# A fused attention, soft-MoE and MLP kernel: its opening stretch rearranged

## The chip, the cores and the metric

The kernel runs on one core of a Trainium2 chip. The time is device microseconds (us) of one launch. The kernel before has a median of 685.09 us over 3 runs (683.9 to 685.98). The names of the engines are those of the profile: PE is TensorE (PEld its weight loads), DVE VectorE, ACT ScalarE, POOL GpSimd, SP the engine whose queue issues the transfers (DMA).

## The reference

Three layers follow one another. What is computed, cut to its core:

```python
# attention: q, k, v (4, 12, 448, 64); rmsnorm(x, g) = x / sqrt(mean(x*x) + 1e-6) * g
q_n, k_n = rmsnorm(q, g_q), rmsnorm(k, g_k)
scores = q_n @ k_n.T / sqrt(64);  scores -= scores.max(-1)
attn = exp(scores);  attn /= attn.sum(-1) + 1e-9;  x = attn @ v      # -> (1792, 768)
# soft MoE: 8 experts, 4 slots each, phi (768, 32), w1 (8, 768, 1024), w2 (8, 1024, 768)
logits = x @ phi;  d = softmax(logits, axis 0);  c = softmax(logits, axis 1)
h = relu((d.T @ x)[expert] @ w1[expert]);  x = c @ (h @ w2[expert])
# MLP: w_in (768, 2048), w_out (2048, 768), given in 64 bit and narrowed on the chip
h = x @ w_in;  g = max(h, 0) + alpha * min(h, 0);  out = g @ w_out
```

## The kernel before

The 48 heads are worked in 24 pairs; two pairs make a group, and q and k of a group come in one tile `qk` (load_qk, one transfer of 448 KB for q and one for k, two such tiles). For each pair n:

- norm_sum 0 squares q and k on ACT into the tile `sqr` (of which there is one buffer, NSQ = 1), norm_sum 1 sums the squares on DVE. norm_rs makes the inverse roots `y` of a whole group: a logarithm and an exponential on ACT, then four small steps on DVE.
- split_mul writes the normed tile `nf` in three products: k by the gains (w = 1), q by its roots (w = 0), k by its roots (w = 2). The gains `G` are the product of g_q and g_k. split_hi rounds `nf` to 16 bits on ACT, split_lo subtracts that from `nf` (the rest). Which engine does the three products and the two subtractions is in the table "PMUL": before, POOL does all five of every pair. There is one `nf` buffer (NNF = 1), so pair n+1's first product waits for pair n's last subtraction.
- turn transposes the split tile on PE (7 matmuls for q, 7 for k), turned copies it out of PSUM on ACT, and transfers bring a second copy to `qB` and `kB`; twin does the same for q. rowmax_mm (PE) and rowmax (DVE) take the row maxima, turn_m and turned_m put them into a row of `qB`.
- score_mm makes the scores on PE, score the exponentials on ACT (two of each block, three blocks of seven with a rest on POOL or DVE by score_lo), and av the products with v on PE. av_out divides.

While the pairs run, the MoE steps of finished pairs, the fetches of w1 and w2 (`unit<-in_moe_w_dram`) and of w_in, and the narrowing of w_in are put between. After the last pair come the experts, whose weights are read from HBM, and the MLP.

The work of all 24 pairs is a list `plan` of 2374 events, and the tuple ORDER gives their order. Each engine takes its instructions strictly in that order, and the SP queue its transfers too: an instruction that waits holds up all behind it on its engine. Ahead of the plan stand the constants: `ident` (POOL), `stack` and `ident16` (DVE), then setup_constants(0), which writes the constant rows 64 to 66 of `qB[0]` and `kB[0]` on POOL. The first event of the plan is setup_constants(1): DVE copies these rows to the other two `qB` and `kB`, and sets `dT`, `vH` and `vR`.

## Time and profile before

| | us |
|---|---|
| median of 3 runs | 685.09 (683.9 to 685.98) |
| the profiled execution, its own time | 685.34 |
| its span, first to last instruction | 683.6 |
| PE busy in the span | 618.2 |
| DVE busy | 456.5 |
| ACT busy | 367.2 |
| POOL busy | 187.9 |

The span is what the profile shows instruction by instruction; 1.74 us of the profiled time lie outside of it. Times of the trace are us from the span's start. In the rows a group names line, engine, operation, output<-input by the program's names, and shape. "x2" is a count; what stands in brackets is how long the engine sat idle before, and what ended that.

### The profile page before, as it was taken

The numbers are of one execution on the slowest core, as the hardware profiler recorded it, in microseconds if no ns is written. First come the engines' busy times: TensorE is split into PE (matmuls) and PEld (weight loads), VectorE is DVE, ScalarE is ACT, GpSimd is POOL, SyncE is SP. The second block draws the span as 40 slices with busy tenths as digits, with TensorE's granted clock in tenths as the row PEclk, the third lists the DMA queues.
The fourth block names the chain that finished last, engine by engine and source line by source line (L and its number), as shares of the span: only waits on it lengthen the run. The fifth ranks groups of instructions, "written<-read, shape, count | busy, mean of one in ns | idle before, by whom it ended". The sixth has DMA issues, their size and how long they took to land.

```text
span 683.6 us, 14138 instructions
## 1 busy us (share of the span) xinstructions
PE 618.2 (90%) x5670; PEld 478.2 (70%) x5670; DVE 456.5 (67%) x913; ACT 367.2 (54%) x709; POOL 187.9 (27%) x195
## 2 busy tenths in 40 slices
PE   0799998889999999997988468999999999999997
PEld 0367766666767776775333114888899999999997
DVE  5778999898999998853011154999964545454540
ACT  3799998798999997771112223776521111111110
POOL 6967665556648562321010000000000000000000
PEclk9989999999999999999999959999999999999999
DMA  4565677462636523669899999330020101010101
GB/s 138 132 204 181 191 206 210 126 174 62 196 97 189 146 62 98 180 211 423 350 424 423 425 425 423 108 120 0 1 93 1 46 1 47 1 47 0 47 1 46
DMA packets 36240, 106.89 MB, mean 156 GB/s; under 512 B 5448, under 2 KB 22352, under 8 KB 31824
## 3 DMA queue, kind: packets, MB, share of 16 engines
q1 hardware_dynamic: 36176, 106.01, 44.4%
q8 instruction: 44, 0.72, 0.5%
q14 instruction: 20, 0.16, 0.1%
HBM read 92.18 MB, written 5.51 MB: 143 GB/s over the span
## 4 chain that ended last, share of the span: by engine, by line
PE 61%; ACT 16%; DMA 9%; DVE 6%; POOL 4%; issue 3%; SPq 0%; DVEq 0%; ACTq 0%; POOLq 0%
PE psa L1491 12%; PE psa L1492 12%; PE psa L1490 11%; DMA unit<-in_moe_w_dram 7%; PE psn L783 5%; PE psv L843 3%; ACT e L799 3%; PE psv L833 3%; PE psa L1332 2%; PE psr L765 2%; PE psa L1303 2%; ACT psn L804 2%; ACT sp L688 2%; POOL nf L682 2%; ACT e L797 1%
## 5 line engine op out<-in xcount | busy, mean ns | idle before, releaser
L1490 PE MATMUL psa<-whi,gh 128*128 128x384 f32 (+1 forms) x448 | 152.0, 339 | 0.0
L1491 PE MATMUL psa<-wlo,gh 128*128 128x384 f32 (+1 forms) x448 | 151.1, 337 | 0.0
L1492 PE MATMUL psa<-whi,gl 128*128 128x384 f32 (+1 forms) x448 | 150.8, 337 | 0.0
L774 DVE TENSOR_REDUCE m<-psr 128x1 f16<-128x448 f32 x168 | 97.5, 615 | 5.7 <-PE psr L765 5.5
L1459 ACT CAST gh<-t 128x512 fp32r<-128x512 f32 x40 | 24.9, 621 | 123.0 <-DVE t L1456 122.5
L1492 PEld LDWEIGHTS psa<-whi,gl 128*128 128x128 f32 x448 | 84.1, 188 | 2.8
L1491 PEld LDWEIGHTS psa<-wlo,gh 128*128 128x128 f32 x448 | 84.2, 188 | 2.7
L1490 PEld LDWEIGHTS psa<-whi,gh 128*128 128x128 f32 x448 | 84.2, 188 | 2.7
L843 PE MATMUL psv<-vH,e 128*128 128x65 f16 (+1 forms) x1152 | 84.8, 195 | 0.0
L843 PEld LDWEIGHTS <-e 128*128 128x128 f16 (+1 forms) x1728 | 80.1, 106 | 0.0
L1453 DVE TENSOR_SCALAR t<-pst,alpha_t 128x256 f32<-128x256 f32 x80 | 34.9, 477 | 62.9 <-PE pst L1447 62.9
L815 POOL TENSOR_TENSOR e<-ef,e 128x448 f16<-128x448 f32 x48 | 53.3, 1111 | 81.3 <-ACT ef L804 60.2
L833 PEld LDWEIGHTS psv<-vR,e 128*128 128x128 f32 (+1 forms) x384 | 59.5, 178 | 20.7 <-issue 11.4
L843 PE MATMUL psv<-vL,e 128*128 128x64 f16 (+1 forms) x576 | 73.0, 194 | 0.0
L799 ACT ACTIVATE e<-psn 128x448 f16<-128x448 f32 x120 | 65.1, 542 | 13.1 <-PE psn L783 10.6
L783 PE MATMUL psn<-q,k 128*128 128x448 f16 (+1 forms) x192 | 62.9, 370 | 9.1 <-ACT ef L804 3.1
L833 PE MATMUL psv<-vR,e 128*128 128x65 f32 (+1 forms) x384 | 70.2, 264 | 0.2 <-PE psn L783 0.2
L783 PE MATMUL psn<-qB,kB 67*128 67x448 f16 (+1 forms) x192 | 62.4, 365 | 1.2 <-DMA qB<-mr 1.2
L765 PE MATMUL psr<-k,q 128*128 128x448 f16 (+1 forms) x192 | 59.1, 383 | 3.8 <-ACT k L717 2.8
L695 POOL TENSOR_TENSOR sp<-nf,sp 128x448 f16<-128x448 f32 x48 | 50.2, 1055 | 12.1 <-ACT sp L688 10.7
L815 DVE TENSOR_TENSOR e<-psn,e 128x448 f16<-128x448 f32 x72 | 44.3, 616 | 13.2 <-ACT psn L804 12.9
L710 PE MATMUL pst<-ident,sp 128*128 128x128 f16 x336 | 28.2, 232 | 17.5 <-POOL sp L695 17.4
(170 smaller groups left out, 1069.6 us busy)
## 6 DMA issues: line engine op xcount, KB each, us to landing
unit<-in_moe_w_dram SPq DMA_DIRECT2D x26, 1536.0 KB, 16.4
unit<-in_moe_w_in_dram SPq DMA_DIRECT2D x24, 512.0 KB, 5.7
rawo<-in_moe_w_out_dram SPq DMA_DIRECT2D x8, 1536.0 KB, 14.5
unit<-in_moe_w_dram SPq DMA_DIRECT2D x36, 256.0 KB, 5.1
qk<-in_q_dram SPq DMA_DIRECT2D x12, 448.0 KB, 3.9
qk<-in_k_dram SPq DMA_DIRECT2D x12, 448.0 KB, 5.8
out_dram<-osb SPq DMA_DIRECT2D x14, 384.0 KB, 2.3
vR<-in_v_dram SPq DMA_DIRECT2D x24, 128.0 KB, 3.9
```

The lines of the kernel that those rows point to most:

```text
L695: eng.tensor_tensor(out=d["sp"][:, a, :, D:], in0=d["nf"][:, a], in1=d["sp"][:, a, :, 0:D], op=ALU.subtract)
L765: nc.tensor.matmul(pn[o0:o1, :S], d["q"][:, c0 : c0 + o1 - o0], d["k"][:, h * S : (h + 1) * S], start=True, stop=True)
L774: nc.vector.tensor_reduce(out=d["m"][:, c : c + 1], in_=d.pop(("pn", c))[:, :S], axis=AX.X, op=ALU.max)
L783: nc.tensor.matmul(pe[o0:o1, :S], lhs[:, c0 : c0 + o1 - o0], rhs[:, h * S : (h + 1) * S], start=st_, stop=not st_,)
L799: nc.scalar.activation(e2[:, 0], pe[:, :S], AF.Exp, scale=0.125)
L815: eng.tensor_tensor(out=e2[:, 1], in0=ef, in1=e2[:, 0], op=ALU.subtract)
L833: nc.tensor.matmul(pv[o0:o1, slot, :], d["e", c][:, qs], d["vv"][:, h, sl * D : 4 * D + 1], start=(j == 0), stop=False,)
L843: nc.tensor.matmul(pv[o0:o1, slot, 0:wd], d["e", c][:, w // 2, qs], (vl if w == 1 else vh)[:, 4 * h + sl, 0:wd], start=(j == 0 and w == 0) ...
L1453: nc.vector.tensor_scalar(out=t0[:, cs], in0=ph[:, cs], scalar1=0.0, scalar2=alpha_t[:, f // 2, i : i + 1], op0=ALU.min, op1=ALU.mult)
L1490: nc.tensor.matmul(a, gh[f][:, ms], hi[:, hs], start=(f == 0 and not (packed and m % 2 == 1 and hf == 0)), stop=False)
L1491: nc.tensor.matmul(a, gh[f][:, ms], lo[:, hs], start=False, stop=False)
L1492: nc.tensor.matmul(a, gl[f][:, ms], hi[:, hs], start=False, stop=(f == KF - 1 and not (packed and m % 2 == 0 and hf == 1)))
```

## The change

Six things are changed.

1. PMUL_OF: all five split steps of pair 0 go to DVE. Pairs 1 to 23 stay on POOL.
2. The constant rows of `qB[0]` and `kB[0]` are written by DVE. The two other copies are made by four small transfers on the SP queue. `vH` and `vR` are set in an event of their own (part 2), `dT` and `stack` in another (part 3), both later in the order.
3. NSQ is 2: two `sqr` buffers.
4. The gains g_q and g_k are fetched first, on ACT's queue, no longer between the two `qk` groups on SP's.
5. NWARM = 12 events of 4 matmuls each on constants (`ident16` by 256 columns of `ident`), into a PSUM buffer that nothing reads. 6 of these events stand ahead of the first transposes.
6. ORDER has 14 more events (2 of constants, 12 of the matmuls). Its first 405 events are in another order (419 with the new ones); from there to the end it is the same.

```diff
-    NSQ = 1
+    NSQ = 2
+    NWARM = 12
...
-    nc.vector.tensor_reduce(
-        out=stack[:, 0, :], in_=ident.rearrange("p (g s) -> p s g", g=4), axis=AX.X, op=ALU.add
-    )
-    for r in range(1, 4):
-        nc.vector.tensor_copy(stack[:, r, :], stack[:, 0, :])
...
             r = qB[0]
-            nc.gpsimd.memset(r[D : D + 3], FC_C)
+            nc.vector.memset(r[D : D + 3], FC_C)
...
-            fc_rows(nc.gpsimd, 0)
-            return
-        got.add("const")
-        for ts in (qB, kB):
-            for t in ts[1:]:
-                if ts is qB or FCS[1] == FCS[2] == FCS[0]:
-                    nc.vector.tensor_copy(t[D : D + 3], ts[0][D : D + 3])
...
+            fc_rows(nc.vector, 0)
+        elif part == 1:
+            got.add("const")
+            for ts in (qB, kB):
+                for t in ts[1:]:
+                    nc.sync.dma_start(t[D : D + 3], ts[0][D : D + 3])
+            nc.sync.dma_start(phi_sb, phi.rearrange("(t p) s -> p t s", p=P))
+        elif part == 2:
+            for t in vH:
...
+            got.add("const v")
+        else:
+            nc.vector.memset(dT[:, S : 4 * P + D], 0.0)
+            nc.vector.tensor_reduce(
...
+    def warm_up(i):
+        if not warm:
+            warm.append(psv())
+        for _ in range(4):
+            nc.tensor.matmul(warm[0][:, : 2 * P], ident16, ident.bitcast(F16), start=True, stop=True)
...
+    def PMUL_OF(n):
+        return {0: ()}.get(n, T["PMUL"][n % 2])
...
-        eng = nc.gpsimd if w in T["PMUL"][n % 2] else nc.vector
+        eng = nc.gpsimd if w in PMUL_OF(n) else nc.vector
...
+        gqk = small.tile([P, 2, D], F32, tag="gqk", name="gqk", bufs=1)
+        nc.scalar.dma_start(gqk[:, 0, :], g_q.rearrange("(o d) -> o d", o=1).to_broadcast([P, D]))
+        nc.scalar.dma_start(gqk[:, 1, :], g_k.rearrange("(o d) -> o d", o=1).to_broadcast([P, D]))
         setup_constants(0)
...
-        gqk = small.tile([P, 2, D], F32, tag="gqk", name="gqk", bufs=1)
-        nc.sync.dma_start(gqk[:, 0, :], g_q.rearrange("(o d) -> o d", o=1).to_broadcast([P, D]))
```

Three places in the engines' order show what moved.

On DVE, at the opening, before: the last constants, then the sums of squares (L641, into `u`), the four small steps of the roots (L654 to L661), the next two sums and the first row maxima (L774).

```order
L582 MEMSET vR_123 64x2x64
L583 MEMSET vR_123 64x2x64
L584 MEMSET vR_123 128x4
L641 TENSOR_REDUCE u<-sqr 128x2x7 x2
L654 TENSOR_SCALAR u<-u 128x28
L657 TENSOR_TENSOR t<-y 128x28
L659 TENSOR_TENSOR t<-t,u 128x28
L661 SCALAR_TENSOR_TENSOR y<-t,y 128x28
L641 TENSOR_REDUCE u<-sqr 128x2x7 x2
L774 TENSOR_REDUCE m<-psr 128x1 x6
```

The same place now (line numbers are those of the changed kernel, L650 the sums, L694 the products, L707 the subtractions):

```order
L441 CAST ident_76<-ident 128x128
L694 TENSOR_TENSOR nf<-qk,G 128x448
L650 TENSOR_REDUCE u<-sqr 128x2x7 x3
L663 TENSOR_SCALAR u<-u 128x28
L666 TENSOR_TENSOR t<-y 128x28
L668 TENSOR_TENSOR t<-t,u 128x28
L670 SCALAR_TENSOR_TENSOR y<-t,y 128x28
L694 TENSOR_TENSOR nf<-qk,y 128x448
L694 TENSOR_TENSOR nf<-nf,y 128x448
L650 TENSOR_REDUCE u<-sqr 128x2x7
L707 TENSOR_TENSOR sp<-nf,sp 128x7x64 x2
```

The `vH` and `vR` constants now stand behind the last of these rows, a third sum stands ahead of the first roots, and the five split steps of pair 0 are DVE's.

On ACT, at the opening, before: squares (L639), logarithm and exponential of the roots (L651, L652), rounding (L688), copies of the transposed q and k (L717).

```order
L639 ACTIVATE sqr<-qk 128x896 x2
L651 ACTIVATE y<-u,eps 128x28
L652 ACTIVATE y<-y 128x28
L688 CAST sp<-nf 128x7x64
L639 ACTIVATE sqr<-qk 128x896
L688 CAST sp<-nf 128x7x64
L639 ACTIVATE sqr<-qk 128x896
L717 COPY q<-pst_208 128x896
L717 COPY k<-pst_228 128x896
```

And now (L648 squares, L660 and L661 roots, L700 rounding, L729 copies):

```order
L648 ACTIVATE sqr<-qk 128x896 x3
L660 ACTIVATE y<-u,eps 128x28
L661 ACTIVATE y<-y 128x28
L648 ACTIVATE sqr<-qk 128x896
L700 CAST sp<-nf 128x7x64 x2
L660 ACTIVATE y<-u,eps 128x28
L661 ACTIVATE y<-y 128x28
L729 COPY q<-pst_227 128x896
L729 COPY k<-pst_240 128x896
```

The third square, which needs group 1's `qk`, stands ahead of the first roots, and the second group's roots ahead of the first copies.

On the SP queue, some 25 transfers in, before: `kB` and `qB` are the second copies, `qB<-mr` the row maxima, `q<-q` the twin, `unit` the 512 KB pieces of w_in.

```order
L719 DMA kB_117<-k 64x896
L738 DMA qB_114<-mr 1x7x128
L605 DMA qk<-in_q_dram 128x2x448
L605 DMA qk<-in_k_dram 128x2x448
L624 DMA vR_123<-in_v_dram 64x2x256
L485 DMA unit<-in_moe_w_in_dram 128x1024 x2
L726 DMA q<-q 64x896
L719 DMA kB_113<-k 64x896
L721 DMA qB_112<-q 64x896
L738 DMA qB_116<-mr 1x7x128
L485 DMA unit<-in_moe_w_in_dram 128x1024 x2
```

And now:

```order
L482 DMA unit<-in_moe_w_in_dram 128x1024
L750 DMA qB_110<-mr 1x7x128
L738 DMA q<-q 64x896
L482 DMA unit<-in_moe_w_in_dram 128x1024
L613 DMA qk<-in_k_dram 128x2x448
L731 DMA kB_109<-k 64x896
L733 DMA qB_108<-q 64x896
L633 DMA vR_119<-in_v_dram 64x2x256
L613 DMA qk<-in_q_dram 128x2x448
L482 DMA unit<-in_moe_w_in_dram 128x1024
L738 DMA q<-q 64x896
L750 DMA qB_112<-mr 1x7x128
```

The first piece of w_in now stands ahead of pair 1's row maxima (`qB_110` here, `qB_114` before), and single pieces stand between the small transfers where two stood together.

## Rows read from the trace of the kernel before

**Rows 1.** Busy time by stretch: engines with instruction counts, PE clock, DMA share, GB/s.

```profile
core 0: us, PE busy (x) PEld busy (x) DVE busy (x) ACT busy (x) POOL busy (x), PEclk, DMA share, GB/s
0.00:5.67 5.67, 0.00 (x0) 0.00 (x0) 3.33 (x8) 1.28 (x1) 4.77 (x13) 1.00 0.53 168
5.67:34.60 28.93, 13.43 (x67) 6.56 (x68) 18.43 (x45) 17.17 (x31) 21.79 (x26) 0.97 0.47 127
34.60:44.16 9.56, 8.87 (x77) 5.64 (x76) 7.32 (x15) 8.29 (x18) 7.11 (x8) 0.72 0.74 234
44.16:60.00 15.84, 15.28 (x210) 11.59 (x207) 12.52 (x27) 15.81 (x36) 10.73 (x11) 1.00 0.74 234
60.00:100.00 40.00, 39.33 (x505) 28.50 (x504) 39.38 (x74) 39.97 (x81) 26.30 (x25) 1.00 0.58 168
100.00:320.00 220.00, 206.16 (x2719) 150.16 (x2717) 188.97 (x403) 183.73 (x380) 111.92 (x107) 0.98 0.54 163
320.00:420.00 100.00, 76.39 (x569) 30.87 (x573) 25.58 (x68) 20.45 (x30) 5.32 (x9) 0.90 0.98 411
...
```

**Rows 2.** Timeline of the opening: start, duration, engine, line, operation.

```profile
5.67 0.95 ACT L639 ACTIVATE sqr<-qk 128x896 f32<-128x896 f32 x1 [3.66 <-DMA qk<-in_k_dram]
...
7.01 0.69 DVE L570 COPY kB<-kB 3x896 f16<-3x896 f16 x2 [1.48 <-POOL kB L553]
7.77 0.17 DVE L576 MEMSET dT<- 128x128 f32 x1
7.92 0.07 DVE L578 MEMSET vH<- 128x8 f16 x1
...
8.43 0.32 POOL L1169 TENSOR_TENSOR G<-gqk 128x64 f32<-128x64 f32 x1 [1.45 <-DMA gqk<-in_g_k_dram]
...
9.45 1.09 DVE L641 TENSOR_REDUCE u<-sqr 128x14 f32<-128x896 f32 x1
10.57 0.95 ACT L639 ACTIVATE sqr<-qk 128x896 f32<-128x896 f32 x1 [3.94 <-DVE u L641]
...
13.72 0.19 DVE L661 SCALAR_TENSOR_TENSOR y<-t,y 128x28 f32<-128x28 f32 x1
...
15.78 2.17 POOL L695 TENSOR_TENSOR sp<-nf,sp 128x448 f16<-128x448 f32 x2
...
18.02 1.13 POOL L682 TENSOR_TENSOR nf<-qk,G 128x448 f32<-128x448 f32 x1
```

**Rows 3.** Timeline of ACT around the first exponentials.

```profile
34.60 0.53 ACT L797 ACTIVATE e<-psn 128x448 f32<-128x448 f32 x1
...
38.50 0.54 ACT L799 ACTIVATE e<-psn 128x448 f16<-128x448 f32 x1 [0.94 <-PE psn L783]
...
43.22 0.94 ACT L717 COPY q<-pst 128x896 f16<-128x896 f16 x1
```

**Rows 4.** Groups of PE, 16 to 28 us: count, busy, mean ns, idle before.

```profile
L765 PE MATMUL psr<-k,q 128*128 128x448 f16 x9 | 4.1, 552 | 1.7 <-ACT k L717 1.7
```

**Rows 5.** Groups of PE, 33 to 39.9 us.

```profile
L783 PE MATMUL psn<-q,k 128*128 128x448 f16 x4 | 2.3, 569 | 0.3 <-ACT e L797 0.3
```

**Rows 6.** Groups of PE, 39.9 to 60 us.

```profile
L783 PE MATMUL psn<-q,k 128*128 128x448 f16 x14 | 4.9, 352 | 0.7 <-ACT ef L804 0.4 <-DVE e L815 0.3
```

**Rows 7.** Busy time of one short stretch, columns as in rows 1.

```profile
36.00:37.00 1.00, 1.00 (x12) 1.00 (x11) 0.98 (x2) 0.88 (x2) 1.00 (x2) 0.50 0.78 204
```

**Rows 8.** The chain that ended last, its longest waits: start, us, what.

```profile
63.62 2.14 DMA qB<-q
101.36 5.03 DMA qB<-mr
...
141.78 6.98 DMA q<-q
```

**Rows 9.** Transfer rate in the first 6 us, in 40 slices.

```profile
GB/s 0 0 0 0 0 0 0 0 0 0 0 0 119 119 48 36 131 155 323 382 370 311 358 454 323 311 406 394 394 394 382 416 318 120 45 21 7 22 9 9
```

**Rows 10.** The page's costliest groups, columns as in rows 4.

```profile
L815 DVE TENSOR_TENSOR e<-psn,e 128x448 f16<-128x448 f32 x72 | 44.3, 616 | 13.2 <-ACT psn L804 12.9
```

## What the change will do to the time: the prediction

> **What bounds the kernel now.** I read the busy time by stretch first [rows 1]. From 60 to 100 us ACT works 39.97 of 40 us, DVE 39.38, PE 39.33: in the steady run of the pairs three engines are full. From 100 to 320 us PE has 206.16 of 220 and the rest is near it. From 320 to 420 us the weights set the pace (DMA share 0.98, 411 GB/s). Nothing of the change lies behind about 70 us, so it can only set how early the full stretch starts. Before 60 us there is room: from 5.67 to 34.60 us ACT works 17.17 of 28.93 us, DVE 18.43, PE 13.43, POOL 21.79.
>
> Second, the timeline of the opening [rows 2]. It is one chain of waits. ACT squares pair 0 when k lands (5.67 to 6.62 us). DVE could sum it at 6.62, but copies and sets constants (7.01 to 9.41; the first of these copies waits for POOL's memsets), so the sum starts at 9.45. With one `sqr` buffer the second square waits for that sum (idle 3.94, start 10.57). Roots are ready at 13.91; POOL's five split steps of pair 0 end at 17.95, and its first product of pair 1 starts at 18.02, because there is one `nf` buffer.
>
> Third, ACT at the first exponentials [rows 3]: they start at 34.60, and the copy that ends at 44.16 closes a set of work that I come back to. Between, ACT works 8.29 of 9.56 us [rows 1], so 1.27 us are idle, 0.94 of them for scores on PE.
>
> Fourth, PE's clock. From 33 to 39.9 us a matmul of 448 columns takes 569 ns; a stretch in it has the granted clock 0.50, the 1.2 GHz level [rows 5, 7]. Behind 39.9 us it takes 352 ns [rows 6]. From 16 to 28 us it takes 552 ns [rows 4], though the clock column reads 0.97 over this part [rows 1]; the durations put it at the lower level too. Before it PE had done nothing.
>
> **The change part by part.** All on the axis of this execution.
>
> *Opening chain.* (a) Constants: a DVE memset of 128 columns takes 0.17 us and one of 8 columns 0.07 [rows 2], so 0.8 ns a column. Now on DVE: three over 896 columns (0.8 us each), one over 448 (0.43), four over 128 (0.17): 3.5 us. With the cast they end near 5.2 us, before k lands at 5.67, and the sums no longer wait for them. A two-byte memset may be faster; the sum doesn't change. (b) Two `sqr` buffers: squares at 5.67 and 6.62, end 7.57. (c) DVE: product with G 5.7 to 6.3 (a product over 448 columns taken at the 616 ns of DVE's subtraction [rows 10]); sums from 6.65, 1.09 each [rows 2], end 8.83. (d) The third square stands ahead of the roots and needs group 1's `qk`. Its 0.92 MB now follow group 0's directly. At 394 GB/s [rows 9] that is 2.3 us; the rate is back at that level at some 4 us, group 0 is through at 5, so group 1 lands near 7.5 to 8.5; I take 8.2. Square to 9.15, logarithm and exponential next to DVE's third sum (9.15 to 10.24), four small steps of 0.19 [rows 2]: roots at 11.1. (e) DVE's two products to 12.35, a sum to 13.45, two subtractions to 14.65 (ACT's roundings lie beside). POOL starts pair 1 at 14.7 instead of 18.02: **-3.3 us**. If group 1 lands only at 9.2, or G's gains late (G waited until 8.43 [rows 2]), it is -2.3; if at 7.5, the second sum of pair 0 decides, not the square, and it is -3.6.
>
> What hides the rest: DVE's five steps for POOL's are 5 x 0.62 = 3.1 us, with the memsets 6.6 us more; what goes are the copies of the constant rows, 0.69 us for two [rows 2], 1.4 for four: 5.2 us net. DVE's idle time up to 60 us is 2.3 + 10.5 + 2.2 + 3.3 = 18.4 us [rows 1], so they fit. DVE's product with G is a new wait (for the gains, over POOL); behind it on DVE stand the three sums, and the roots wait for these, which is the late case in (d). The four small transfers of constant rows wait only for memsets that are done by then.
>
> *Pairs 1 to 4.* POOL's five steps a pair are as before, so the 3.3 us pass on. Between, ACT has the square of pair 5 ahead of a rounding of pair 2; it needs group 2's `qk`, whose transfer follows POOL's products of pair 1 and so moves by 3.3 too. Now the set: up to the copy ending at 44.16 ACT has done 6 squares, 3 root pairs, 10 roundings, 8 copies of q and k, 2 of maxima, 2 of v, and the exponentials of 7 blocks (2 single, 5 double). Counted off in the new order, ACT holds the same set up to its own eighth copy. So the two can be compared there: the start moves by 3.3, and of the 1.27 us that ACT idles behind 34.60 between none and all goes. I take half, **-0.6**, as the new order brings more score matmuls ahead of the exponentials that need them.
>
> *Matmuls on constants.* 256 columns cost half of the spacing of 448 at the lower level, some 0.2 us. The 24 ahead of the first transposes take 5 us, from about 5.2 on, while PE has nothing else: the first transposes wait for the split (from 15.78 us on before [rows 2]). The 8 behind the transposes lie beside two ACT copies. The other 16 stand between row maxima, 0.8 us per event at the lower level, where PE works 13.43 of 28.93 us: 0, at worst +1.7 if two of the four events delay a maximum that DVE waits for.
>
> The Trainium skill, "TensorE: Matmul & The Clock Gate", section Part 1, says that the lower clock is the default and activity releases it. The rows agree that PE starts low (552 ns) and is high behind 39.9 us. By that rule the extra matmuls could lift the opening; I hold it for a rival, since PE idles again between its 24 matmuls and the first transposes.
>
> *The gains on ACT's queue.* They leave SP's queue, which is what lets group 1 follow group 0 (in the sum above). The same skill, "DMA: Bandwidth & Descriptors", section Issuing engines are not separate DMA queues, says such transfers share the engines and interleave. By that k would land later by the gains' 64 KB; at 394 GB/s [rows 9] this is 0.2 us, and the sum would be -3.7. No row here has a transfer on ACT's queue.
>
> *Sum.* -3.3 - 0.6 = -3.9 us of the profiled 685.34 us (span 683.6 and 1.74 outside). The profiled execution lies 0.25 above the median, so I set it against the median: 685.09 - 3.9 = 681.2 us, written 681.3. The gain must live to the end: behind 44 us ACT is full, so work done earlier stays earlier; the long waits at 101.36 and 141.78 us [rows 8] come from transfers issued in an unchanged order and move along; the weights' stretch starts as pairs free the buffers.
>
> **The rivals.** About 2 us (0.3%) is what a measurement can tell from no change here.
>
> A, faster still: PE holds 2.4 GHz from the first transposes on. Speaks for it the 552 against 352 ns. Then all 1.27 us of ACT's idle goes, and two sets of 7 transposes in the opening shorten by some 0.35 each: -3.3 - 1.3 - 0.7 = -5.3, 679.8 us. Against: PE's gap between 10 and 14 us. Chance 0.18.
>
> B, no measurable change: DVE sets the start of the full stretch, not ACT. To be 3.9 us earlier with 5.2 us more work, its idle time up to there must fall from 18.4 to 9.3 us. If it falls to 12.5 only, 18.4 - 12.5 - 5.2 = 0.7 of gain is left: 684.4. For it: DVE is 39.38 of 40 us full from 60 us on [rows 1]. Against: most of its idle time lies in the opening, in the waits that go. Chance 0.15.
>
> C, slower: the pieces of w_in now stand ahead of pair 1's and pair 2's row maxima and twin on SP's queue. If one of these small transfers then waits as long as the twin at 141.78 (6.98 us [rows 8]), with all engines behind it, the time is 681.3 + 7.0 = 688.3. It decides from a wait of 6 us on; at 5.03 (as at 101.36) the outcome is still no change. For it: three such waits stand in the chain [rows 8]. Against: the DMA share is 0.74 in this stretch [rows 1] and there were pieces among the small transfers before, with no such wait ahead of 63.62. Chance 0.12.
>
> **How the numbers follow.** The forecast has 0.55, A 0.18, B 0.15, C 0.12. The forecast's own range, from -2.3 with no idle regained and a late event of matmuls (+0.8) to -3.6 - 1.3, is 680.2 to 683.6. A reaches from there to 678.0 if a rise of the clock also saves waits that the rows don't show. Up, B ends near 685 and the small waits of C at 686. The range 677.8 to 686.0 leaves out most of C and a little of A. Faster by over 0.3% (below 683.0) is nearly all of the forecast, A, and little of B: 0.71. Slower (above 687.1) is C with its long wait: 0.12. The rest, 0.17.
>
> **What would show it.** In the changed profile: DVE's first sum near 6.7 us; roots near 11.1; POOL's first product of pair 1 near 14.7; ACT's first exponential near 30; the same set of ACT's work done near 40.3; the row for 60 to 100 us as full as before; the waits on `qB<-mr` and `q<-q` near 97 and 138 us with like lengths. The clock: matmuls of 448 columns still near 550 ns in the opening by the forecast, near 350 by A. The forecast is wrong if the third square starts later than 9.2, if ACT idles for a piece of data that the new order brings too late, or if a gain at 40 us is not there at 100.

## The result, and the profile after

| | median, us | ratio to before, 95% interval |
|---|---|---|
| before, same chip (5 runs) | 683.9 (681.78 to 685.98) | 1 |
| after (5 runs) | 690.91 (688.51 to 693.7) | 1.0102 [1.0062, 1.0141] |

The change makes the kernel 1.0% slower, some 7 us. The forecast was 3.9 us faster, with a range that ended at 686.0. The profiled execution of after took 689.68 us (span 687.9).

The opening first. The next rows are the timeline of after, as in [rows 2] and [rows 3].

```profile
6.72 4.30 PE L593 MATMUL psv<-ident,ident 128*128 128x256 f16 x24 [6.72 <-DVE ident L441]
8.21 0.32 POOL L1186 TENSOR_TENSOR G<-gqk 128x64 f32<-128x64 f32 x1 [6.90 <-DMA gqk<-in_g_k_dram]
9.60 1.79 ACT L648 ACTIVATE sqr<-qk 128x896 f32<-128x896 f32 x2 [6.65 <-DMA qk<-in_k_dram]
12.38 0.95 ACT L648 ACTIVATE sqr<-qk 128x896 f32<-128x896 f32 x1 [0.99 <-DMA qk<-in_k_dram]
14.88 0.19 DVE L670 SCALAR_TENSOR_TENSOR y<-t,y 128x28 f32<-128x28 f32 x1
17.18 1.15 DVE L707 TENSOR_TENSOR sp<-nf,sp 128x448 f16<-128x448 f32 x2
18.46 1.13 POOL L694 TENSOR_TENSOR nf<-qk,G 128x448 f32<-128x448 f32 x1 [9.93 <-DVE vH L570]
27.98 0.95 ACT L648 ACTIVATE sqr<-qk 128x896 f32<-128x896 f32 x1 [1.87 <-DMA qk<-in_k_dram]
34.58 0.54 ACT L809 ACTIVATE e<-psn 128x448 f32<-128x448 f32 x1
43.35 0.96 ACT L729 COPY q<-pst 128x896 f16<-128x896 f16 x1
```

The two squares run back to back, as they should with two buffers, but the first starts at 9.60 instead of 5.67: group 0's k lands 3.9 us later. Roots end at 15.07, and POOL starts pair 1 at 18.46, not at 14.7 (before: 18.02). The first exponential starts at 34.58 (34.60 before), and the eighth copy ends at 44.31 (44.16 before). So there was no gain at 44 us, and up to there only 0.15 us had been lost. The loss comes behind it. The next rows are after by stretch, columns as in [rows 1]:

```profile
5.67:34.60 28.93, 16.86 (x104) 10.94 (x105) 21.62 (x48) 16.33 (x28) 13.49 (x15) 0.75 0.49 136
34.60:44.16 9.56, 9.11 (x66) 4.79 (x65) 8.85 (x17) 9.13 (x21) 8.71 (x10) 0.87 0.70 204
44.16:60.00 15.84, 14.33 (x214) 10.89 (x211) 13.87 (x25) 14.01 (x30) 8.47 (x8) 1.00 0.69 207
60.00:100.00 40.00, 36.50 (x447) 25.55 (x445) 38.25 (x72) 36.81 (x76) 25.62 (x25) 1.00 0.54 158
320.00:420.00 100.00, 79.98 (x590) 32.14 (x589) 26.24 (x75) 20.89 (x30) 5.30 (x9) 0.83 0.98 409
```

From 44.16 to 100 us ACT was idle 0.06 us before; now it is idle 1.83 + 3.19 = 5.0 us. In the chain that ended last (start, us, what; compare [rows 8]) after has these waits:

```profile
2.25 10.03 DMA qk<-in_k_dram
22.30 5.65 DMA qk<-in_k_dram
47.15 5.35 DMA q<-q
85.83 5.02 DMA q<-q
107.42 5.72 DMA qB<-mr
147.12 6.01 DMA q<-q
178.46 7.93 DMA q<-q
```

The first is group 1's k, landed at 12.28 where the forecast had 8.2; the second group 2's k; the third, the fourth and the last are twins of q and have no like in [rows 8]. Around the last one nothing is lost by the ruler that follows (2.8 us at pair 10, 2.9 at pair 12).

**A ruler.** DVE divides each pair's sums once, a subtraction `X<-psv,z`. Its start marks how far the kernel is. These are pairs 0 to 3 in before, and then in after:

```profile
49.72 0.61 DVE L863 TENSOR_TENSOR X<-psv,z 128x448 f32<-128x448 f32 x1
58.72 0.62 DVE L863 TENSOR_TENSOR X<-psv,z 128x448 f32<-128x448 f32 x1
70.66 0.61 DVE L863 TENSOR_TENSOR X<-psv,z 128x448 f32<-128x448 f32 x1
81.47 0.61 DVE L863 TENSOR_TENSOR X<-psv,z 128x448 f32<-128x448 f32 x1
```

```profile
50.23 0.62 DVE L875 TENSOR_TENSOR X<-psv,z 128x448 f32<-128x448 f32 x1
60.43 0.62 DVE L875 TENSOR_TENSOR X<-psv,z 128x448 f32<-128x448 f32 x1
74.63 0.62 DVE L875 TENSOR_TENSOR X<-psv,z 128x448 f32<-128x448 f32 x1
86.71 0.61 DVE L875 TENSOR_TENSOR X<-psv,z 128x448 f32<-128x448 f32 x1
```

Shift of after against before: 0.5, 1.7, 4.0, 5.2 us. For every kernel run the same ruler gives, in us, its profiled execution less that of before. The last column is the ratio of the timed runs to those of before in the same series, with its 95% interval; it need not equal the quotient of two medians.

| kernel | pair 0 | 1 | 2 | 3 | pair 9 | last pair | timed runs, ratio |
|---|---|---|---|---|---|---|---|
| after | 0.5 | 1.7 | 4.0 | 5.2 | 3.0 | 1.5 | 1.0102 [1.0062, 1.0141] |
| before_again | -0.4 | -0.4 | -0.4 | -0.4 | -0.4 | -1.9 | |
| gains_back | -0.5 | 0.6 | 2.8 | 3.9 | 1.6 | 1.1 | 1.0074 [1.0041, 1.0107] |
| gains_row | -1.6 | -0.5 | 1.7 | 3.0 | 1.1 | -0.4 | 1.0034 [1.0009, 1.0058] |
| gains_act | 1.0 | 1.0 | 1.0 | 1.0 | 4.2 | 4.4 | 1.0023 [0.9991, 1.0055] |
| old_order | 4.4 | 4.4 | 4.5 | 4.4 | 1.7 | 0.4 | 1.006 [1.0031, 1.0088] |
| old_order_gains | 2.6 | 2.6 | 2.6 | 2.6 | -0.1 | -1.9 | 1.0034 [1.0003, 1.0065] |
| no_warm | 0.4 | 1.4 | 3.8 | 5.9 | 4.3 | 4.2 | 1.0099 [1.007, 1.0129] |
| hybrid_early | -2.0 | -2.0 | -2.0 | -2.0 | -3.2 | -5.1 | **0.9933 [0.9907, 0.996]** |
| hybrid_row | -0.2 | -0.3 | -0.3 | -0.3 | -3.6 | -4.8 | 0.997 [0.9944, 0.9997] |
| cut_second | 0.8 | 0.8 | 0.8 | 0.8 | -3.3 | -4.8 | 0.9994 [0.997, 1.0018] |
| cut_third | 2.2 | 5.3 | 5.3 | 5.2 | 5.8 | 4.2 | 1.0053 [1.0028, 1.0078] |
| hybrid_pool | -4.1 | -4.1 | -4.1 | -4.1 | -1.4 | -2.9 | 0.9979 [0.995, 1.0007] |
| stack_early | -3.4 | -2.1 | 0.1 | 1.6 | 1.0 | -0.5 | 1.0052 [1.003, 1.0074] |
| pieces_later | -0.9 | 0.2 | 2.5 | 3.7 | 2.2 | 0.8 | 1.0029 [1.0001, 1.0058] |
| twins_early | 4.6 | 5.8 | 8.0 | 9.4 | 7.8 | 6.4 | 1.0135 [1.0105, 1.0166] |
| maxima_early | 4.5 | 5.7 | 7.9 | 9.0 | 5.5 | 3.9 | 1.0098 [1.0069, 1.0128] |
| maxima_late | -5.3 | -2.2 | -2.2 | -2.3 | -6.4 | -8.2 | 0.9985 [0.9957, 1.0013] |

Before_again is the kernel before, profiled once more: it differs from its first profile by 0.4 us at pairs 0 to 3, by 3.3 at pair 6 and by 1.9 at the last pair. So of a single profile only the first pairs are read here, and a total only from the timed runs.

Even the place of pair 0 holds chance, through the clock. Two kernels of the experiments below, gains_row and cut_second, have the same 209 first events, pair 0's exponentials among them. The first of these starts at 32.22 us in gains_row and at 31.44 in cut_second, the last at 40.03 and 40.60. Between them, from 36 to 38 us, the granted clock reads 1.00 in gains_row and 0.50 in cut_second. A score matmul of each, gains_row first:

```profile
37.02 0.35 PE L795 MATMUL psn<-q,k 128*128 128x448 f16 x1
```

```profile
37.11 0.58 PE L795 MATMUL psn<-q,k 128*128 128x448 f16 x1
```

So 1.4 of the 2.4 us between the two at pair 0 arise where the order is the same. What a kernel loses from pair 0 to pair 3 is steadier, and the readings below go by that.

From pair 8 to pair 9 most kernels gain 2.3 to 2.4 us on before (gains_act and no_warm do not); there the profile of before has its wait of 6.98 us [rows 8], and before_again gains 2.3 too. In the profile of after the lag is 5.2 us at pair 3, 1.5 at the last pair and 4.3 at the end of the span. So 2.8 us of it arise behind the pairs, where the clock reads 0.83 from 320 to 420 us against 0.90 before; how the timed runs come to 7 us is not traced pair by pair.

### The profile page after: what moved, and what is told of

Its sections match the earlier page's. It is cut to its first block, busy times and chain, and to the rows that moved or that the text cites. A ratio compares the mean times of both kernels' runs of the same rounds, so it can differ in the third digit from the quotient of the medians.

```text
span 687.9 us, 14242 instructions
## 1 busy us (share of the span) xinstructions
PE 625.3 (91%) x5718; PEld 482.2 (70%) x5718; DVE 467.1 (68%) x923; ACT 367.9 (53%) x709; POOL 177.9 (26%) x181
## 4 chain that ended last, share of the span: by engine, by line
PE 63%; DMA 14%; ACT 11%; DVE 7%; issue 2%; POOL 1%; SPq 1%; ACTq 0%; DVEq 0%
PE psa L1508 11%; PE psa L1509 11%; PE psa L1507 11%; DMA unit<-in_moe_w_dram 7%; PE psn L795 5%; PE psv L855 4%; DMA q<-q 4%; PE psv L845 3%; PE psa L1349 2%; PE psr L777 2%; DMA qk<-in_k_dram 2%; PE psa L1320 2%; ACT e L811 2%; PE pst L1464 1%; ACT sp L700 1%
## 5 line engine op out<-in xcount | busy, mean ns | idle before, releaser
L795 PE MATMUL psn<-q,k 128*128 128x448 f16 (+1 forms) x192 | 61.4, 361 | 12.0 <-DMA q<-q 4.8
L795 PE MATMUL psn<-qB,kB 67*128 67x448 f16 (+1 forms) x192 | 61.0, 357 | 1.8 <-DMA qB<-mr 1.8
L777 PE MATMUL psr<-k,q 128*128 128x448 f16 (+1 forms) x192 | 57.1, 366 | 2.0 <-DVE m L786 1.3
L707 POOL TENSOR_TENSOR sp<-nf,sp 128x448 f16<-128x448 f32 x46 | 47.9, 1051 | 19.9 <-ACT sp L700 16.6
L1336 DVE TENSOR_REDUCE hT<-pst 128x16 f32<-128x64 f32 x16 | 3.6, 225 | 58.1 <-PE pst L1334 58.1
```

What stands on the lines that cost most here:

```text
L707: eng.tensor_tensor(out=d["sp"][:, a, :, D:], in0=d["nf"][:, a], in1=d["sp"][:, a, :, 0:D], op=ALU.subtract)
L777: nc.tensor.matmul(pn[o0:o1, :S], d["q"][:, c0 : c0 + o1 - o0], d["k"][:, h * S : (h + 1) * S], start=True, stop=True)
L795: nc.tensor.matmul(pe[o0:o1, :S], lhs[:, c0 : c0 + o1 - o0], rhs[:, h * S : (h + 1) * S], start=st_, stop=not st_,)
```

## The experiments

### The gains: whose bytes delay group 0

The gains reach all 128 partitions as 2 x 128 small pieces. In gains_back they stand on SP's queue behind group 0 again, as before the change; the rest is after.

```diff
-        nc.scalar.dma_start(gqk[:, 0, :], g_q.rearrange("(o d) -> o d", o=1).to_broadcast([P, D]))
-        nc.scalar.dma_start(gqk[:, 1, :], g_k.rearrange("(o d) -> o d", o=1).to_broadcast([P, D]))
...
+        nc.sync.dma_start(gqk[:, 0, :], g_q.rearrange("(o d) -> o d", o=1).to_broadcast([P, D]))
+        nc.sync.dma_start(gqk[:, 1, :], g_k.rearrange("(o d) -> o d", o=1).to_broadcast([P, D]))
```

> The changed kernel with one edit undone: the gains are fetched on SP's queue between the two qk groups, as before. Queue theory (the gains on ACT's queue slow the first q and k): the first square starts at 5.7 us instead of 9.6, POOL's first product of pair 1 at 15 to 16 instead of 18.5, and the pairs are 2.5 to 3.5 us earlier throughout, so that the time is 686 to 688.5 us. Order theory (the new order's transfers put waits on the path between 44 and 90 us, whatever the opening does): the opening is earlier too, but pair 6 is still some 6 us later than in the kernel before and the time stays at 690 to 691.

688.08 us, 1.0074 [1.0041, 1.0107]. The first square is back at 5.50, but the third waits for group 1 until 11.59, and POOL starts pair 1 at 17.67, not at 15 to 16 as the queue theory had it. So the small pieces cost in either place: ahead of group 0 they delay both groups, between the groups the second.

Gains_act is the reverse: before, with only the gains moved to ACT's queue.

```diff
+        nc.scalar.dma_start(gqk[:, 0, :], g_q.rearrange("(o d) -> o d", o=1).to_broadcast([P, D]))
+        nc.scalar.dma_start(gqk[:, 1, :], g_k.rearrange("(o d) -> o d", o=1).to_broadcast([P, D]))
         setup_constants(0)
...
-        nc.sync.dma_start(gqk[:, 0, :], g_q.rearrange("(o d) -> o d", o=1).to_broadcast([P, D]))
-        nc.sync.dma_start(gqk[:, 1, :], g_k.rearrange("(o d) -> o d", o=1).to_broadcast([P, D]))
```

> The kernel before with one part of the change alone: the gains are fetched first, on ACT's queue. Queue theory: the first square starts near 9.6 us instead of 5.7, and the time is 2 to 4 us longer than before (686 to 688). If instead group 0's own transfers are not slowed by it and something else of the change delays them, the first square starts at 5.7 to 6 us and the time is that of before, or up to 1 us shorter since group 1 lands earlier.

684.92 us, 1.0023 [0.9991, 1.0055]: not told apart from before, where the queue theory had 2 to 4 us. In its timeline the first square again comes late:

```profile
9.49 0.95 ACT L639 ACTIVATE sqr<-qk 128x896 f32<-128x896 f32 x1 [6.54 <-DMA qk<-in_k_dram]
```

With nothing else of the change in it, the gains alone make the delay of 3.8 us. DVE's constants, which end at 9.41 in before [rows 2], cover most of it: the first sum starts at 10.47 instead of 9.45, and 1.0 us is what all the first pairs show.

Gains_row keeps queue and place and takes away the pieces: after, with each gain fetched as one row, multiplied on one partition and spread over the others by a matmul with ones.

```diff
-        gqk = small.tile([P, 2, D], F32, tag="gqk", name="gqk", bufs=1)
+        gqk = small.tile([1, 2, D], F32, tag="gqk", name="gqk", bufs=1)
+        nc.scalar.dma_start(gqk[:, 0, :], g_q.rearrange("(o d) -> o d", o=1))
+        nc.scalar.dma_start(gqk[:, 1, :], g_k.rearrange("(o d) -> o d", o=1))
...
-        nc.gpsimd.tensor_mul(G, gqk[:, 0, :], gqk[:, 1, :])
+        nc.gpsimd.tensor_mul(grow, gqk[:, 0, :], gqk[:, 1, :])
+        nc.tensor.matmul(pG[:, :D], ones, grow, start=True, stop=True)
+        nc.vector.tensor_copy(G, pG[:, :D])
```

> The changed kernel, order and all, but the gains come as one row each (2 pieces of 256 bytes instead of 256 pieces, still first and on ACT's queue) and a matmul with a column of ones spreads them over the partitions. If it is the 256 small pieces that slow group 0: first square at 5.5 to 6 us, third square near 8 to 9, POOL's first product of pair 1 near 15, and the pairs start 3 us earlier. If it is ACT's queue as such: first square still near 9.6. By the order theory the loss of 4 to 6 us between pair 0 and pair 4 is there all the same, and the time is 686 to 688.

686.22 us, 1.0034 [1.0009, 1.0058]: 0.7% below after, some 4.6 us. Its timeline:

```profile
5.54 1.79 ACT L648 ACTIVATE sqr<-qk 128x896 f32<-128x896 f32 x2 [2.73 <-DMA qk<-in_k_dram]
9.91 0.95 ACT L648 ACTIVATE sqr<-qk 128x896 f32<-128x896 f32 x1 [2.59 <-DMA qk<-in_k_dram]
15.93 1.14 POOL L694 TENSOR_TENSOR nf<-qk,G 128x448 f32<-128x448 f32 x1 [11.51 <-DVE vH L570]
```

The queue is not to blame, the pieces are: from 3 to 6 us the transfers move 124, 222 and 237 GB/s in after, us by us, and 382, 391 and 369 in gains_row. Whether it is their number, their size of 256 B, or that 128 of them read the same row, no run tells apart. The queue's lines on the two pages (packets, MB, share of 16 engines) are, after first:

```profile
q10 hardware_dynamic: 288, 0.07, 0.0%
```

```profile
q10 hardware_dynamic: 4, 0.00, 0.0%
```

Group 1 lands at 9.81 even so (in the chain its k is issued at 2.26 and takes 7.55), not at 8.2; POOL is 2.1 us earlier than before, not 3.3. This landing differs from profile to profile: in the eleven kernels below and here that have the gains as rows, the square that waits for it starts between 8.93 and 10.20. And the gain does not last: 1.6 us early at pair 0, 3.0 late at pair 3.

### The order: which stretch loses

Old_order has all parts of after but the order of before; the 14 new events (2374 to 2387, of which 2376 and on are the matmuls) stand near the places of what they replace. Old_order_gains puts the gains back on SP's queue as well.

```diff
 ORDER = (
-    969, 2376, 968, 1076, 1796, 2377, 993, 2378,
...
+    2376, 2377, 2378, 2379, 2380, 2381, 968, 992,
...
```

> The changed kernel with all its parts, but with the order of the kernel before, into which only the 14 new events are put (constants of v behind pair 0's last subtraction, the others and the matmuls at about their places of the changed order). Order theory: the waits on the twin and on v between 44 and 90 us go, and the time is 684 to 686, the late first square (9.6 us) still in it. Queue theory alone: the time stays at 688 to 691, since the late first square is what costs.

> Both: the order of before with the 14 new events put in, and the gains back on SP's queue. If the two theories hold together and add up, the opening is 3 us earlier than before (POOL's first product of pair 1 near 15), no new wait follows, and the time is 680 to 682, what I had predicted for the change. If the time is that of before (683 to 685), an earlier opening is worth nothing, because the pairs behind it are paced by something else.

686.77 us, 1.006 [1.0031, 1.0088], and 685.28 us, 1.0034 [1.0003, 1.0065]. Neither time is one that was expected. Both start worse than after, with 4.4 and 2.6 us at pair 0, as they have no early start at all (POOL's pair 1 at 20.49 and 18.24, before 18.02). But the lag stays flat from pair 0 to pair 3, while every kernel with the whole changed order (after, gains_back, gains_row, no_warm) loses 4.4 to 5.5 us there. This suggests the changed order for the opening and that of before for the pairs behind it. Four kernels, all with the gains as rows, have the changed order up to a cut and that of before behind it: to ahead of pair 5's square (hybrid_early, event 94, and with `stack` made in the opening), to pair 0's first score (hybrid_row, 121), pair 1's (cut_second, 209), pair 2's (cut_third, 270). The edit of cut_second, at the cut:

```diff
-    408, 121, 648, 458, 1, 1224, 1508, 145, 1580, 1248, 25, 2375,
...
+    408, 121, 648, 458, 900, 910, 891, 338, 901, 911, 957, 1224,
...
```

> As hybrid_row (681.6), but the order of before begins already at event 94, ahead of pair 5's square, so that this square, which needs group 2's k, stands behind pair 2's rounding as it did before; and dT and stack are set in the opening, as in stack_early. If the 2.2 us that ACT waits there for k were what took the opening's 2.8 us back, pairs 0 to 5 are 2 to 3 us earlier than in the kernel before (in hybrid_row 0.2), and the time is 679 to 680.5. If the wait only moves to a later piece of data, the pairs stand as in hybrid_row and the time is 681 to 682.

> As gains_row, but only the first 121 events, up to the first score matmul, stand in the changed order; from there on the events stand in the order of the kernel before. If the changed order's loss lies behind the first scores, pairs 0 to 8 are all some 3 us earlier than in the kernel before and the time is 680 to 682. If an earlier start is taken back by something else, the pairs fall back to the old pace by pair 4, and the time is 683 to 685.

> The gains as one row each; the changed order up to pair 1's first score matmul, from there the order of before. Measured by the start of DVE's X<-psv,z of each pair against the profile of before. Theory (the loss of 4.6 us between pair 0 and pair 3 of the changed order lies behind pair 1's first score): about -1.5 at pair 0, within 1 us of that at pairs 1 to 3, time near 682. Rival (it is made between the first scores of pair 0 and of pair 1): +1 to +3 at pair 3 as with the whole changed order, time near 686.

> As the last one, but the changed order is kept up to pair 2's first score matmul. Theory (what delays pair 2 is that its last row maximum, their transposition, and its twin are issued late, which this kernel keeps): -1.6, -0.5, near +1.5 at pair 2 and +1.5 to +3 at pair 3, time near 685 to 686. Rival (the loss lies behind pair 2's first score): at most +0.5 at pair 3, time near 683.

679.5 us (0.9933), 681.56 (0.997), 683.46 (0.9994), 687.25 (1.0053): the more of the changed order, the slower, up to this cut; the whole of it is not slower still (gains_row, 1.0034). The largest step is 0.6% between the last two, run on one chip in one series; the intervals do not touch. The stretch between the first scores of pairs 1 and 2 thus costs some 4 us. Cut_second is flat, so its rival fell; but it lies at 0.8 where the theory had -1.5, and the clock is a part of that (above). Cut_third loses 3.1 us, though between pairs 0 and 1, ahead of where either side had it. Hybrid_row's time is in the range expected of an early start, but its pairs are at -0.2 and not at -3.

Hybrid_early is faster than before by 0.67% [0.4, 0.93], some 4.6 us, and so than after. In its timeline there is an early start of the kind that the forecast had asked for, 2.1 us at POOL (18.02 before), 3.0 at the first exponential (34.60), 2.0 at each of the first pairs:

```profile
15.95 1.13 POOL L694 TENSOR_TENSOR nf<-qk,G 128x448 f32<-128x448 f32 x1 [11.49 <-DVE vH L570]
26.54 0.95 ACT L648 ACTIVATE sqr<-qk 128x896 f32<-128x896 f32 x1
31.62 0.53 ACT L809 ACTIVATE e<-psn 128x448 f32<-128x448 f32 x1
```

Its square of pair 4 waits for no transfer. In the changed order pair 5's square is issued earlier, ahead of a rounding of pair 2, when group 2's k has not landed; after idles 1.87 us there (row at 27.98), gains_row 2.04. What this square alone is worth is not settled: hybrid_row, which keeps it early, and hybrid_early, which has `stack` in the opening besides, have intervals that overlap.

What the later loss looks like, by stretch, columns as in [rows 1]: gains_row first, then cut_third.

```profile
44.16:60.00 15.84, 14.28 (x185) 9.75 (x183) 13.96 (x28) 13.22 (x30) 6.35 (x6) 1.00 0.68 211
```

```profile
44.16:60.00 15.84, 13.30 (x118) 9.18 (x117) 11.08 (x23) 10.03 (x21) 5.66 (x7) 0.74 0.69 221
...
48.00:52.00 4.00, 1.82 (x14) 0.77 (x12) 2.79 (x5) 1.96 (x5) 2.67 (x3) 0.97 0.77 231
52.00:56.00 4.00, 3.95 (x34) 3.12 (x35) 2.65 (x5) 2.35 (x5) 2.42 (x3) 0.50 1.04 358
56.00:60.00 4.00, 4.00 (x31) 2.93 (x29) 1.87 (x6) 2.05 (x6) 0.48 (x1) 0.50 0.11 24
```

ACT, full before (15.81 of 15.84), is idle 2.62 us in gains_row; its exponentials there wait for scores (line engine operation, count, busy, mean ns, idle before):

```profile
L811 ACT ACTIVATE e<-psn 128x448 f16<-128x448 f32 x8 | 4.5, 559 | 1.3 <-PE psn L795 1.3
L809 ACT ACTIVATE e<-psn 128x448 f32<-128x448 f32 x2 | 1.1, 544 | 1.3 <-PE psn L795 1.0 <-PE psv L845 0.4
```

DVE is fuller in this stretch than before: 13.96 us in gains_row and 13.87 in after, against 12.52 [rows 1]. In cut_third a lull of PE (1.82 of 4 us busy), in which its matmuls for the maxima wait for DVE's maxima (three waits, 2.2 us in all from 44 to 56 us), is followed by a granted clock of 0.50, the 1.2 GHz level, with PE busy 7.95 of the next 8 us; so a part of its 3.1 us between pairs 0 and 1 is the clock. In gains_row the clock reads 1.00 from 44 to 60 us and the loss is there too.

### The order: which instructions

Four attempts to name the instruction, all on gains_row, and one on hybrid_early. Numbers in the diffs are events.

Twins_early: the twins of pairs 2 and 3 (1342, 1343), a transfer each on SP's queue, directly behind their transposes.

```diff
-    1318, 457, 0, 673,
+    1318, 1342, 457, 0, 673,
```

> As gains_row (changed order), but the twin transfers of pairs 2 and 3 are issued right behind the copies of their q and k, some 120 and 160 events earlier than in the changed order. If the waits on the twin at 45 and 62 to 70 us are themselves what the changed order costs, pairs 2 to 4 are 3 to 5 us earlier than in gains_row and the time is 682 to 684. If they stand for all that comes late there (the row maxima of the same pair, or v behind them, are due at the same place), the wait is taken over by the maxima's transfer and the gain is under 1 us: 685.5 to 686.5.

693.33 us, 1.0135 [1.0105, 1.0166]. Worse: pair 3's twin is issued at 45.56, after SP's queue has waited 2.8 us for the second copy of pair 3's q, and all behind it waits too; pair 2's row maxima follow at 53.91 (47.61 in gains_row). Besides, group 3's k, issued ahead of this twin and at about the same time as in gains_row (38.28), lands late; ACT's next squares start at 45.09, in gains_row at 43.37. Why it lands late is not shown. In the chain:

```profile
38.55 6.52 DMA qk<-in_k_dram
```

Stack_early: the event (2375) that makes `stack` and `dT` on DVE, in the opening instead of between scores.

```diff
-    992, 1797, 1016,
+    992, 2375, 1797, 1016,
```

> As gains_row, but the event that sets dT and stack (5 small DVE steps, 3.1 us long at 43 us in the changed kernel, beside POOL's work) stands in the opening, between two sums, where DVE waits and POOL has nothing. If these 3.1 us hold up DVE's row maxima and with them the scores of pair 1, pairs 1 to 4 are 2 to 3 us earlier and the time is 683.5 to 685. If the wait on the twin at 45 us, which begins behind it, is set by the transfers ahead of it on SP's queue, nothing is gained: 685.5 to 686.5.

686.93 us, 1.0052 [1.003, 1.0074]; 5.0 us are lost from pair 0 to pair 3. So `stack` and `dT` are not the cause.

Pieces_later: group 4's transfers and a piece of w_in behind pair 2's maxima.

```diff
-    1105, 842, 75, 1652, 974, 818, 1990, 99, 49,
+    1105, 75, 1652, 974, 818, 99, 49,
```

> As gains_row (changed order), but the two large transfers that stand right ahead of pair 2's twin and row maxima on SP's queue (448 KB of group 4's q, 512 KB of w_in) are issued right behind these. If the 0.96 MB ahead is what the wait of 5.2 us at 45 us consists of, the wait shrinks to some 2 us, pair 2 is 2.5 to 3 us earlier than in gains_row (at -1 instead of 1.7 us against the kernel before), and the time is 683 to 685 as far as no later wait takes it. If the twin simply comes too late in the changed order, the wait stays over 4 us and the time at 686.

684.85 us, 1.0029 [1.0001, 1.0058]. The time is in the range of the first theory, but against before it is no gain on gains_row (1.0034), and pair 2 is at 2.5, not at -1. The wait of 5.2 us on a twin near 45 us is gone from its chain, and still 4.6 us are lost from pair 0 to pair 3. So that wait is not what makes the loss.

Maxima_early: of pair 2, the last two row maxima, their transposition, the copy of it and the twin earlier (49 instead of 13 events between the copy and pair 2's first score). Maxima_late: hybrid_early with the last three of these later (21 events instead of 75).

```diff
-    578, 794, 1809, 2180,
+    578, 1342, 794, 1809, 2180,
```

> The whole changed order with the gains as rows, but five events of pair 2 earlier: the last two row maxima, their transposition, the copy of it and the twin, the copy now 49 events ahead of pair 2's first score matmul instead of 13. Theory (late maxima of pair 2 make the loss between pairs 1 and 2, 2.2 of the 4.6 us): -1.6, -0.5, then -0.5 to 0 at pair 2, time 683 to 684. Rival (the order around them does it, with these five events or without): +1.7 at pair 2 and +3.0 at pair 3, time 686.

> The best kernel so far (gains as rows, changed order up to ahead of pair 5's square, then that of before), with three events of pair 2 issued later: its twin 33 events ahead of its first score matmul instead of 94, its maxima's transposition and the copy of it 23 and 21 ahead instead of 77 and 75. Theory (late maxima of pair 2 make the loss): -2.0 at pairs 0 and 1, then -0.5 to +0.5 from pair 2 on, time 681 to 682. Rival (they have nothing to do with it): -2.0 at pairs 0 to 3, time 679.5.

690.9 us, 1.0098 [1.0069, 1.0128], and 684.09 us, 0.9985 [0.9957, 1.0013]. The theory found no support: early maxima did not bring the loss down (4.5 us still go from pair 0 to pair 3). But the edit also brought in a wait of its own, and pair 0 is later by 6.1 us: PE's matmuls for pair 2's maxima now wait for the twin that was moved ahead of them.

```profile
42.25 1.06 PE L777 MATMUL psr<-k,q 128*128 128x448 f16 x3 [3.77 <-DMA q<-q]
```

Late maxima show pair 0 at -5.3, and 3.1 us given back in one wait on a twin:

```profile
42.66 7.64 DMA q<-q
```

How much of the -5.3 is the order is not shown: the clock reads 1.00 from 28 to 44 us in this profile, and 0.50 and 0.75 from 32 to 36 and 36 to 40 us in that of hybrid_early. By the ratios late maxima are 0.5% worse than hybrid_early, but their runs spread from 677.54 to 687.92, and the profiled one is the fastest of them.

### The matmuls, the split, and chance

No_warm is after without the 48 matmuls on constants.

```diff
-    NWARM = 12
+    NWARM = 0
```

> The changed kernel without the 48 matmuls on constants (12 events left out, all else as in the change). If they only fill idle time, as I had costed them, the pairs stand within 0.5 us of the changed kernel's and the time is 690 to 691. If they keep the clock up, it is 1 to 3 us longer; if they hold up the row maxima behind them, 1 to 2 us shorter.

691.82 us, 1.0099 [1.007, 1.0129], against 1.0102 with them: no difference that these runs, good to some 2 us, can tell. The clock is higher with them in places. Groups of PE from 12 to 28 us, after and no_warm:

```profile
L777 PE MATMUL psr<-k,q 128*128 128x448 f16 (+1 forms) x13 | 4.0, 402 | 0.7 <-DVE m L786 0.7
```

```profile
L776 PE MATMUL psr<-k,q 128*128 128x448 f16 (+1 forms) x10 | 4.4, 558 | 1.9 <-ACT k L728 1.1 <-DVE m L785 0.7
```

Some of after's matmuls for the maxima run at the higher level there; PE waits for others in this stretch, and pair 0 ends at the same time.

Hybrid_pool is hybrid_early with pair 0's split on POOL, as before.

```diff
-        return {0: ()}.get(n, T["PMUL"][n % 2])
+        return T["PMUL"][n % 2]
```

> As hybrid_early (679.5), but pair 0's five split steps are POOL's again, as in the kernel before. DVE's five steps took 3.1 us where POOL's take some 5, so if the split on DVE is what the opening gains, POOL's first product of pair 1 stands 2 us later (at 17 to 18 us), pairs 0 to 5 likewise, and the time is 681 to 682. If the gain comes from the gains' one row, the second square buffer and the constants alone, the time stays at 679 to 680.

681.18 us, 0.9979 [0.995, 1.0007]. POOL starts pair 1 at 15.91, not later than with the split on DVE (15.95):

```profile
9.24 0.95 ACT L648 ACTIVATE sqr<-qk 128x896 f32<-128x896 f32 x1 [1.91 <-DMA qk<-in_k_dram]
15.91 1.18 POOL L694 TENSOR_TENSOR nf<-qk,G 128x448 f32<-128x448 f32 x1
```

But in this profile group 1 landed earlier, and the square that waits for it starts at 9.24 instead of 9.93. From this square to POOL's start are 6.67 us here, and 6.0 to 6.1 in each of the ten kernels that have the gains as rows and the split on DVE. So the split on DVE brings POOL's start forward by some 0.6 us, not by the 2 us expected; most of the early start comes from the other parts. The first pairs are even earlier here (-4.1), with the clock at 0.85 from 32 to 36 us and at 1.00 behind it, where hybrid_early has 0.50 and 0.75. The ratios lean to DVE by 0.5%, with intervals that overlap: what moving the split is worth in time is not settled.

> The kernel before, a second profile. It tells how much of a difference between two profiles is chance: the times of the pairs to 0.5 us if the order alone sets them, the stretch behind the pairs to 1 or 2 us, as far as the clock falls in other places. Both theories expect the pairs within 0.5 us.

683.45 us, one run. It set the limits for reading the ruler, above.

## Why the prediction was wrong

**Opening chain, (d), and "The gains on ACT's queue": the step that failed first.** The forecast had k land at 5.67 as before and priced the gains at 64 KB of rate, 0.2 us. Measured: 3.9 us for after (9.60), 3.8 in gains_act, nothing in gains_row (5.54). I divided bytes by a rate that rows showed for large transfers; with 2 pieces of 256 B in place of 256 the delay is gone. The Trainium skill, "DMA: Bandwidth & Descriptors", section Issuing engines are not separate DMA queues, says that such transfers share the engines; the runs agree with the sharing, but the price that I made of it was 20 times too small. In the changed kernel this is worth 0.7%, some 4.6 us (1.0102 against 1.0034 in gains_row).

**(d), the second part.** Without the pieces group 1 lands at 9.81 in gains_row, 1.6 us behind the 8.2 of the sum. The text's own late case (9.2) gave -2.3; gains_row and hybrid_early have -2.1 at POOL. Over the ten kernels with the gains as rows and the split on DVE, POOL starts pair 1 between 14.95 and 16.23, on average at 15.5. So the term -3.3 was -2.5 on average, and between -1.8 and -3.1.

**(a), (b), (e).** The memsets had their price (0.81 us for 896 columns; those of two bytes were no faster), but four are over 896 columns, not three, and gaps of 0.24 us lie between them. They and the cast ended near 6.7, not 5.2, hidden by the late k, and in gains_row by group 1's landing (DVE idles 1.45 us ahead of the third sum). The second buffer did what was said. POOL's start followed from DVE's last subtraction as worked out (18.33, then 18.46). But by hybrid_pool DVE's five steps bought only some 0.6 us there.

**The -0.6.** From 34.60 to 44.16 us, 9.56 us in all, ACT idles 0.43 us in after and not 1.27. This was no gain: from 5.67 to 44.16 us ACT has 25.46 us of work in both kernels, and after only did behind 34.60 what it had not done ahead of it (16.33 us against 17.17). In hybrid_early, with its start 3.0 us early, ACT idles 2.3 us up to its eighth copy, which ends 1.9 us early (42.23). So the term was nothing in the one and of the other sign in the other.

**"Pairs 1 to 4", "so the 3.3 us pass on": the step that failed second.** With the pairs in before's order, pairs 0 to 3 do keep one shift: flat in old_order, old_order_gains, hybrid_early, hybrid_row and cut_second. From POOL's start to pair 0 even that order does not keep it: hybrid_early has -2.1 and -2.0, but hybrid_row -2.8 and -0.2 and cut_second -2.6 and 0.8, the clock being a part of this. In the changed order it fails twice. Pair 5's square waits for group 2's k; I saw that square, and priced it as moving along with POOL's products, without the 5.65 us from that transfer's issue to its landing. And from pair 0 to pair 3 another 4 to 5 us go. I counted that ACT's set up to its eighth copy was the same in both orders; it was, and it ended only 0.15 us later than before, at 44.31. But the set says nothing of how far PE, DVE and POOL are, and in gains_row it was PE's scores that ACT then waited for.

**Matmuls on constants: 0.** Right by no_warm to the 2 us that it can tell, though the clock was higher for some matmuls. Rival A's rise was there in part, without a gain.

**The rivals.** B was not met as it stood: hybrid_early has the same added work on DVE and gains 0.67%. But in the changed order DVE is fuller behind 44 us than before, and whether the order loses by DVE was not tested. C had the right sign, and a twin's wait is there (5.35 us at 47.15). But pieces_later took the two large transfers right ahead of that twin away, and the loss stayed; so that the time went C's way is not shown to be for C's reason.

**What stays open.** By the ratios, the order loses some 4 us between the first scores of pairs 1 and 2 (cut_third less cut_second), and hybrid_early less cut_second says about as much for events 94 to 209, of which the wait of pair 5's square is one part seen. Which instructions of the later stretch do it is not shown: twins, `stack`, large transfers and maxima were each moved, and none brought the loss down, though the moves of twins and maxima made new waits of their own. That it is the interleaving of PE's scores with other work, as ACT's waits for `psn` suggest, or DVE's late maxima, for which PE waits in cut_third, is argued only.

**What was right.** An early start with before's order behind it (hybrid_early) is 0.67% faster than before; the forecast's sum was 0.57%. That the two are so near is in part luck. POOL starts 2.1 us early, not 3.3; pairs 0 to 3 are 2.0 us early; what makes the rest of the 4.6 us behind them is not traced. What was sound is that the opening has room and that an earlier start can be worth time at the end; the kernel that was given did not have that start.

## What to carry to other kernels

Price a transfer by its pieces as well as its bytes, above all ahead of the first load on which everything waits; a vector that all partitions need can come as one row. When an order is changed for the sake of its beginning, keep it only to where the gain is made, and judge the rest by a marker that comes once per block of work on the last engine, not by one engine's set of work, and by more than one profile, as chance moved that marker by over 1 us where the events were the same. And when a wait is named the cause, take it away alone: here the loss went on when the wait on the twin was gone.

## What the runs showed of the hardware

- 256 pieces of 256 B on one queue, 64 KB in all, delayed the landing of the first k on another queue by 3.9 us (9.60 in after against 5.67 before) and by 3.8 with nothing else changed (9.49 in gains_act); 2 pieces of 256 B delayed it by nothing (5.54 in gains_row).
- Some small steps of DVE last until POOL's instruction beside them is over. In after, the same line takes 0.17 us with POOL idle and 0.80 beside POOL's product, and it ends at 20.53, within 0.05 us of that product. A memset of 128 columns beside the same product takes 0.17 us, so not all of them do this:

```profile
14.36 0.17 DVE L663 TENSOR_SCALAR u<-u 128x28 f32<-128x28 f32 x1
...
19.55 0.94 POOL L694 TENSOR_TENSOR nf<-qk,y 128x448 f32<-128x448 f32 x1
...
19.63 0.17 DVE L575 MEMSET vR<- 64x128 f32 x1
19.73 0.80 DVE L663 TENSOR_SCALAR u<-u 128x28 f32<-128x28 f32 x1
```

- A lull of PE in a busy stretch (cut_third, idle 2.18 of the 4 us from 48 to 52) was followed by 8 us at a granted clock of 0.50, the 1.2 GHz level, though PE was busy for 7.95 of them.
